# A fused linear-attention and mixture-of-experts kernel: unpermuted decay tiles, split copies and long probability rows in the first chunk

## The chip, the cores and the metric

The kernel runs on one core of one Trainium2 chip. The metric is device microseconds (us) of one execution; a profiled execution also has a span, about 1.7 us shorter, measured from the core's first instruction to its last. Engines: PE = TensorE (matmul), PEld = its weight load, DVE = VectorE, ACT = ScalarE, POOL = GpSimd, SP = SyncE, which here only issues DMA transfers. Runs over 1.5% above the fastest of the same kernel are called slow.

## The reference, cut to what matters

```python
f = 1 / (1 + exp(-f_logit))                       # q, k, v, f_logit: 4 x 8 x 768 x 48
for t in range(768):                               # per batch and head
    state = f[t][:, None] * state + outer(k[t], v[t])
    y[t] = q[t] @ state
x = y, heads side by side                          # 3072 x 384
p = domain_probs / (domain_probs.sum(-1) + 1e-9)   # 3072 x 4
out = sum_e p[:, e] * (relu(x @ w1[e]) @ w2[e])    # w1: 4 x 384 x 1024, w2: 4 x 1024 x 384
```

## The kernel before

The sequence is cut into six chunks of 128 positions; each chunk has 4 batches. Attention of a chunk feeds the expert matmuls of the same chunk. A list planner in Python orders all work by estimated costs and emits it; the chip then runs each engine's list in that order. The first expert matmul ("first MoE matmul" below) needs the transposed attention output of all four batches of chunk 0, and the first expert weight. The parts that matter here:

```python
# loads of chunk 0, one per tensor and batch, 192 KB each, all issued by SyncE, in this order
"f0 k0 q0 f1 k1 q1 f2 f3 k2 q2 v0 k3 q3 v1 v2 v3"
...
def load_w(i, e, which):                           # eight weight loads, issued by GpSimd
    ins["w", i] = nc.gpsimd.dma_start(out=w[:, e], in_=r[e])
    if i == 0:
        after(ins["w", 0], ins[0, "k", B - 1])     # released by the last key load
...
def load_p(c):                                     # six small loads, 16-byte pieces
    nc.sync.dma_start(out=p_dst[:, :, c], in_=p_src[:, :, c])
...
for o in done:                                     # fillers keep TensorE busy until the MoE starts
    for _ in range(o.pad):
        nc.tensor.matmul(out=spare[:, 0:256], lhsT=busy[:, 0:128], rhs=busy, start=True, stop=True)
    o.emit(o.engine)
```

## Time and profile before

| | before |
|---|---|
| median of the first 3 runs | 303.09 us (301.59 to 309.10) |
| profiled run, span | 302.06 us, 300.4 us |
| TensorE busy | 290.7 us (97%) |
| first weight lands | 23.05 us |
| first MoE matmul | 23.10 us |
| all timed runs of this kernel (g_before_again apart) | 56; 17 of them over 307 us |

The table reads as a start of 23.1 us, then an almost gapless run of TensorE.

### The profile page before, as it was taken

To read this page: it belongs to the slowest core of one execution; us is meant where nothing else is said; L and a number is where in the kernel's file an instruction comes from. 1 tells how busy PE (TensorE), PEld (TensorE's weight loads), DVE (VectorE), ACT (ScalarE), POOL (GpSimd) and SP (SyncE) were. 2 spreads that over 40 slices of the span, in tenths; PEclk is the share of its full clock that TensorE was granted. 3 is DMA by queue.
4 is the path that set the end of the run, shared out by engine and by line. 5 is a ranking of instruction groups with operands and counts; after the bars stand their busy time and mean duration, and the time that the engine had idled before them with its cause. 6 is when DMAs were issued, how large, how long until landed. Compare 5 with 4: busy or idle time off the path is not lost.

```text
span 300.4 us, 5514 instructions
## 1 busy us (share of the span) xinstructions
PE 290.7 (97%) x2111; PEld 168.1 (56%) x2141; DVE 135.8 (45%) x268; ACT 172.5 (57%) x300; POOL 95.7 (32%) x157
## 2 busy tenths in 40 slices
PE   7799999999999999999999999999999999999995
PEld 5564555567775565555555555555555555555553
DVE  6784013787852675516465325454415343201223
ACT  5766654858875455677355576445475444475440
POOL 4484400408756048423426243522432000000000
PEclk9999999999999999999999999999999999999999
DMA  7999999964994679969796978201322201200002
GB/s 155 210 180 206 207 207 200 220 103 71 224 208 103 119 142 180 196 136 156 152 177 116 241 147 153 49 21 34 94 58 52 48 13 41 75 4 2 0 0 105
DMA packets 137354, 36.08 MB, mean 120 GB/s; under 512 B 128496, under 2 KB 135792, under 8 KB 137328
## 3 DMA queue, kind: packets, MB, share of 16 engines
q1 hardware_dynamic: 131568, 29.45, 50.5%
q0 software_dynamic: 5760, 6.29, 12.6%
q8 instruction: 16, 0.26, 0.4%
q14 instruction: 10, 0.08, 0.1%
HBM read 31.51 MB, written 4.72 MB: 121 GB/s over the span
## 4 chain that ended last, share of the span: by engine, by line
PE 90%; DMA 4%; SPq 3%; DVE 1%; issue 1%
PE ps_m L356 42%; PE ps_m L344 41%; SPq L222 3%; DMA w_sb<-in_moe_w_dram 3%; PE ps_t L300 2%; DMA k<-in_k_dram 1%; PE ps_t L315 1%; PE ps_t L311 1%; PE ps_t L321 1%; PE ps_t L255 1%; PE ps_t L285 1%; DVE Sf L328 0%; DVE o L367 0%; DVE yb L218 0%; PE ps_t L340 0%
## 5 line engine op out<-in xcount | busy, mean ns | idle before, releaser
L356 PE MATMUL ps_m<-w_sb,h 128*128 128x384 bf16 x776 | 153.1, 324 | 0.2
L344 PE MATMUL ps_m<-xT,w_sb 128*128 128x512 bf16 (+1 forms) x594 | 150.8, 362 | 2.4 <-DMA w_sb<-in_moe_w_dram 0.5
L352 ACT ACTIVATE h<-ps_m 128x512 bf16<-128x512 f32 (+1 forms) x169 | 97.2, 577 | 96.5 <-PE ps_m L344 91.8
L356 PEld LDWEIGHTS <-h 128*128 128x128 bf16 x776 | 73.6, 98 | 58.7
L363 DVE SCALAR_TENSOR_TENSOR o<-ps_m,pn,o 128x384 f32<-128x384 f32 (+1 forms) x73 | 44.6, 611 | 107.3 <-PE ps_m L356 102.7
L344 PEld LDWEIGHTS <-w_sb 128*128 128x128 bf16 x624 | 59.5, 98 | 46.8 <-issue 0.8
L276 POOL TENSOR_TENSOR qk<-q,e 128x384 bf16<-128x384 f32 x19 | 22.8, 1202 | 67.3 <-ACT e L262 64.8
L335 POOL TENSOR_TENSOR Sf<-Sf,egs 48x192 f32<-48x192 f32 x40 | 20.1, 502 | 47.1 <-DVE Sf L328 45.1
L350 DVE TENSOR_SCALAR h<-ps_m 128x512 bf16<-128x512 f32 (+1 forms) x39 | 21.9, 578 | 27.6 <-PE ps_m L344 25.2
L304 DVE TENSOR_TENSOR AT<-ps_t,mask 128x512 bf16<-128x512 f32 x48 | 30.2, 682 | 6.8 <-PE ps_t L300 6.8
L276 POOL TENSOR_TENSOR qk<-k,e 128x384 bf16<-128x384 f32 x20 | 21.9, 1093 | 10.7 <-ACT egs L266 6.6
L262 ACT ACTIVATE e<-ps_t 128x384 f32<-128x384 f32 x24 | 20.8, 865 | 3.6 <-PE ps_t L255 2.5
L328 DVE TENSOR_TENSOR Sf<-Sf,ps_t 48x192 f32<-48x192 f32 x40 | 14.0, 350 | 8.3 <-PE ps_t L321 7.4
L336 POOL CAST sb<-Sf 48x192 bf16<-48x192 f32 x40 | 13.6, 339 | 2.6
L365 ACT ACTIVATE o<-ps_m,pn 128x384 f32<-128x384 f32 x20 | 11.6, 580 | 4.4 <-PE ps_m L356 3.2
L569 PE MATMUL ps_m<-busy 128*128 128x256 bf16 x69 | 12.1, 319 | 1.3 <-DVE busy L140 1.3
L264 ACT ACTIVATE e<-ps_t 128x384 f32<-128x384 f32 x24 | 13.0, 542 | 0.0
L247 ACT ACTIVATE ex<-f 128x768 f32<-128x768 f32 (+1 forms) x14 | 10.5, 750 | 4.4 <-DMA f<-in_f_logit_dram 4.4
L315 PE MATMUL ps_t<-vb,AT 128*128 128x48 bf16 x192 | 11.4, 184 | 1.0 <-DVE vb L218 1.0
L218 POOL CAST vb<-v 128x384 bf16<-128x384 f32 x18 | 9.4, 540 | 8.5 <-DMA v<-in_v_dram 7.3
L315 PEld LDWEIGHTS <-AT 128*128 128x128 bf16 x192 | 9.8, 97 | 3.1 <-issue 1.1
L251 ACT ACTIVATE gp<-ex 128x768 bf16<-128x768 f32 (+1 forms) x14 | 10.5, 752 | 0.4
(50 smaller groups left out, 134.5 us busy)
## 6 DMA issues: line engine op xcount, KB each, us to landing
w_sb<-in_moe_w_dram POOLq DMA_DIRECT2D x8, 768.0 KB, 18.9
out_dram<-o SPq DMA_DIRECT2D x23, 192.0 KB, 2.1
f<-in_f_logit_dram SPq DMA_DIRECT2D x10, 384.0 KB, 4.3
k<-in_k_dram SPq DMA_DIRECT2D x10, 384.0 KB, 5.5
q<-in_q_dram SPq DMA_DIRECT2D x10, 384.0 KB, 5.4
v<-in_v_dram SPq DMA_DIRECT2D x10, 384.0 KB, 5.1
f<-in_f_logit_dram SPq DMA_DIRECT2D x4, 192.0 KB, 4.0
k<-in_k_dram SPq DMA_DIRECT2D x4, 192.0 KB, 4.1
```

Of the source, the lines that this page charges most:

```text
L262: nc.scalar.activation(out=e[:, 0].rearrange("t (d h) -> t h d", d=D), in_=cs[:, 0:HD].rearrange("t (i r d) -> t r i d", r=2, d=D), func=A ...
L276: engines[eng].tensor_tensor(out=tl("qk", c, b)[:, j, :, 0:D].rearrange("t (i r) d -> t i r d", r=2), in0=tl("qk"[j], c, b // 2)[:, hh(b), ...
L304: nc.vector.tensor_tensor(out=tl("AT", c, b)[:, r].rearrange("s i t -> s (i t)"), in0=tl("A", c, b, r).rearrange("s i t -> s (i t)"), in1= ...
L315: nc.tensor.matmul(out=y[:, h * D:(h + 1) * D], lhsT=AT[:, r, i, :], rhs=vb[:, h, :], start=(c == 0), stop=True, skip_group_check=True)
L328: nc.vector.tensor_tensor(out=Sf[rows, b], in0=Sf[rows, b], in1=KV[rows, :, r, :], op=ALU.add)
L335: nc.gpsimd.tensor_tensor(out=Sf[rows, b], in0=Sf[rows, b], in1=eg, op=ALU.mult)
L336: nc.gpsimd.tensor_copy(out=nb[rows, b, :, r * D:(r + 1) * D], in_=Sf[rows, b])
L344: nc.tensor.matmul(out=tl("hp", c, e, fc, n0)[:, n0:n1], lhsT=w1_sb[:, e, kk, fc * 128:(fc + 1) * 128], rhs=tl("xT", c)[:, kk, n0:n1], sta ...
L350: nc.vector.tensor_relu(out=dst, in_=src)
L352: nc.scalar.activation(out=dst, in_=src, func=AF.Relu)
L356: nc.tensor.matmul(out=tl("op", c, e, nt, part)[:, cols], lhsT=tl("h", c, e)[:, fc, nt * T:(nt + 1) * T], rhs=w2_sb[:, e, fc, cols], start ...
L363: nc.vector.scalar_tensor_tensor(out=o, in0=op, scalar=pe, in1=o, op0=ALU.mult, op1=ALU.add)
```

## The change

Its intent is to shorten the attention of chunk 0 and to replace the six small probability loads. The release of the weights by the last key load stays as it was.

```diff
-    nc.sync.dma_start(out=p_dst[:, :, c], in_=p_src[:, :, c])          # six times
+    nc.scalar.dma_start(out=praw, in_=moe_domain_probs.rearrange("(r p) e -> r p e", p=T))   # once, at the start
+    nc.tensor.transpose(out=tl("pp")[:, e], in_=praw[:, :, e], identity=ident32)             # x4, fp32
...
-    nc.scalar.activation(out=e[:, 0].rearrange("t (d h) -> t h d", d=D), in_=cs..., func=AF.Exp, scale=-1.0)
+    if c == 0:
+        nc.scalar.activation(out=e[:, 0], in_=cs[:, 0:HD], func=AF.Exp, scale=-1.0)
+    else: ...                                                            # as before
...
-            pe = {"DVE": 0.6, "POOL": 1.0} if c < 2 else {"POOL": 1.0}
+            pe = {"DVE": 0.55} if c == 0 and b == B - 1 else {"DVE": 0.55, "POOL": 1.36} if c == 0 else ...
...   (the last batch's copies of QK, y and xT in two parts, ScalarE and VectorE)
+            parts = [slice(0, KD)] if c or b < B - 1 else [slice(0, 2), slice(2, KD)]
...
-                    add_load(c + 2, nm, 2 * half, 2, u0 + 30 + 4 * half + j)
+                    add_load(c + 2, nm, 2 * half, 2, u0 + 30 + 4 * half + j, deps=[wd[5]])
```

More of the change, by code (lines that the diff above doesn't have):

```diff
@@ L167 @@
         Sb.append(t)
-    pt = const.tile([128, B * C, E], FP32)
-    pn = const.tile([128, B * C, E], FP32)
-    psm = const.tile([128, B * C, 1], FP32)
+    NR = B * C
+    praw = const.tile([NR, T, E], FP32)
+    ident32 = const.tile([NR, NR], FP32)
+    nc.vector.tensor_copy(out=ident32, in_=ident[0:NR, 0:NR])
+    pn = const.tile([T, E, NR], FP32)
+    psm = const.tile([T, NR], FP32)
     w1_sb = wpool.tile([128, E, KD, F], BF16)
@@ L186 @@
         "cs": ([T, 512], FP32), "tp": ([128, 2, NP, T], BF16), "A": ([T, NP, T], FP32), "y": ([T, 512], FP32),
-        "KV": ([T, 512], FP32), "xp": ([T, KD, T], BF16), "hp": ([128, NT], FP32), "op": ([128, 512], FP32),
+        "KV": ([T, 512], FP32), "xp": ([T, KD, T], BF16), "hp": ([128, NT], FP32), "op": ([128, 512], FP32), "pp": ([T, E, NR], FP32),
     }
@@ L192, in tl @@
         if (kind, key) not in tiles:
-            room = kind if kind in rooms else "ps_m" if kind in ("hp", "op") else "ps_t"
+            room = kind if kind in rooms else "ps_m" if kind in ("hp", "op", "pp") else "ps_t"
             slot = P.slot[(room, kind) + key if room.startswith("ps_") else (room,) + key]
@@ L231, in load_w, with load_p, pe_pp, probs @@
             after(ins["w", 0], ins[0, "k", B - 1])
-    p_src = moe_domain_probs.rearrange("(b c p) e -> p b c e", p=128, c=C)
-    p_dst = pt.rearrange("p (b c) e -> p b c e", c=C)
-    def load_p(c):
-        nc.sync.dma_start(out=p_dst[:, :, c], in_=p_src[:, :, c])
-    def probs(c):
-        t, s, n = (x.rearrange("p (b c) e -> p b c e", c=C)[:, :, c] for x in (pt, psm, pn))
-        nc.vector.tensor_reduce(out=s, in_=t, axis=mybir.AxisListType.X, op=ALU.add)
-        nc.vector.tensor_single_scalar(out=s, in_=s, scalar=1e-9, op=ALU.add)
-        nc.vector.reciprocal(out=s, in_=s)
-        nc.vector.tensor_tensor(out=n, in0=t, in1=s.broadcast_to([128, B, E]), op=ALU.mult)
+    def load_p():
+        nc.scalar.dma_start(out=praw, in_=moe_domain_probs.rearrange("(r p) e -> r p e", p=T))
+    def pe_pp():
+        for e in range(E):
+            nc.tensor.transpose(out=tl("pp")[:, e], in_=praw[:, :, e], identity=ident32)
+    def probs():
+        nc.vector.tensor_reduce(out=psm, in_=tl("pp").rearrange("p e r -> p r e"), axis=mybir.AxisListType.X, op=ALU.add)
+        nc.vector.tensor_single_scalar(out=psm, in_=psm, scalar=1e-9, op=ALU.add)
+        nc.vector.reciprocal(out=psm, in_=psm)
+        nc.vector.tensor_tensor(out=pn, in0=tl("pp"), in1=psm.unsqueeze(1).broadcast_to([T, E, NR]), op=ALU.mult)
     def gate1(c, b, n):
@@ L261, in exps @@
         cs, e = tl("cs", c, b), tl("e", c, b)
-        nc.scalar.activation(out=e[:, 0].rearrange("t (d h) -> t h d", d=D), in_=cs[:, 0:HD].rearrange("t (i r d) -> t r i d", r=2, d=D),
-                             func=AF.Exp, scale=-1.0)
+        if c == 0:
+            nc.scalar.activation(out=e[:, 0], in_=cs[:, 0:HD], func=AF.Exp, scale=-1.0)
+        else:
+            nc.scalar.activation(out=e[:, 0].rearrange("t (d h) -> t h d", d=D),
+                                 in_=cs[:, 0:HD].rearrange("t (i r d) -> t r i d", r=2, d=D), func=AF.Exp, scale=-1.0)
         nc.scalar.activation(out=e[:, 1], in_=cs[:, 0:HD], func=AF.Exp)
@@ L274, in product @@
         e = tl("e", c, b)[:, j]
-        e = e.rearrange("t (d r i) -> t i r d", d=D, r=2) if j == 0 else e.rearrange("t (i r d) -> t i r d", d=D, r=2)
+        e = e.rearrange("t (d r i) -> t i r d", d=D, r=2) if j == 0 and c > 0 else e.rearrange("t (i r d) -> t i r d", d=D, r=2)
         engines[eng].tensor_tensor(out=tl("qk", c, b)[:, j, :, 0:D].rearrange("t (i r) d -> t i r d", r=2),
@@ L336, in state, with pe_xt @@
             nc.gpsimd.tensor_copy(out=nb[rows, b, :, r * D:(r + 1) * D], in_=Sf[rows, b])
-    def pe_xt(c, b):
-        for kk in range(KD):
-            nc.tensor.transpose(out=tl("xp", c, b)[:, kk, :], in_=tl("yb", c, b)[:, kk * 128:(kk + 1) * 128], identity=ident)
+    def pe_xt(c, b, ks):
+        for kk in range(ks.start, ks.stop):
+            nc.tensor.transpose(out=tl("xp", c, b, ks.start)[:, kk, :], in_=tl("yb", c, b)[:, kk * 128:(kk + 1) * 128], identity=ident)
     def mm_h(c, e, fc, n0, n1):
@@ L360, in ev_o @@
         op, o = tl("op", c, e, nt, part)[:, cols], tl("o", c, nt)[:, cols]
-        pe = pn[:, nt * C + c, e:e + 1]
+        pe = pn[:, e, nt * C + c:nt * C + c + 1]
         if e > 0:
@@ L416, in attention @@
                        deps=[G[b]], takes=[pt_("cs")], lag=0.2, frees=[("gp", c, half)])
-            ex = P.add(f"exps {c}.{b}", {"ACT": 0.98 if c else 1.1}, on(exps), s(0) + 0.1, deps=[cs],
+            ex = P.add(f"exps {c}.{b}", {"ACT": 0.98 if c else 1.0}, on(exps), s(0) + 0.1, deps=[cs],
                        takes=[("e", c, b)] + ([("egs", c, b)] if c == 0 else []), frees=[pt_("cs")])
@@ L420, in attention @@
                             frees=[("e", c, b)], lag=2.0) if c and more else None)
-            pe = {"DVE": 0.6, "POOL": 1.0} if c < 2 else {"POOL": 1.0}
+            pe = {"DVE": 0.55} if c == 0 and b == B - 1 else {"DVE": 0.55, "POOL": 1.36} if c == 0 else {"DVE": 0.6, "POOL": 1.0} if c == 1 else {"POOL": 1.0}
             qm = P.add(f"q {c}.{b}", pe, one(product, 0), s(4) - 0.2,
@@ L425, in attention @@
                        deps=[ex, ld[c, "k", b]], takes=[("qk", c, b)], frees=[("k", c, half), ("e", c, b)])
-            vb = P.add(f"v {c}.{b}", {"ACT": 0.52, "DVE": 0.36} if c == 0 else {"POOL": 0.5, "ACT": 0.52} if c == 1 else {"POOL": 0.5}, one(cast_v), s(4),
+            vb = P.add(f"v {c}.{b}", {"ACT": 0.52} if c + b == 0 else {"ACT": 0.52, "DVE": 0.36} if c == 0 else {"POOL": 0.5, "ACT": 0.52} if c == 1 else {"POOL": 0.5}, one(cast_v), s(4),
                        deps=[ld[c, "v", b]], takes=[("vb", c, b)], frees=[("v", c, half)])
@@ L432, in attention @@
                            takes=[pt_("tp")], frees=[("qk", c, b)], lag=0.2)
-                et = P.add(f"ev_tp {c}.{b}", {"DVE": 0.69, "ACT": 1.05}, lambda e, b=b: copy(e, tl("QK", c, b)[0:MP], tl("tp", c, b)[0:MP]), s(4) + 0.1,
-                           deps=[tq, tk], takes=[("QK", c, b)], frees=[pt_("tp")])
-            else:
-                et = P.add(f"tp {c}.{b}", {"DMA": 1.8}, on(dma_tp), s(4), deps=[qm, km], takes=[("QK", c, b)],
-                           frees=[("qk", c, b)], lag=2.2)
+                parts = [(slice(0, 2), [tq, tk])] if c or b < B - 1 else [(slice(j, j + 1), [tj]) for j, tj in enumerate((tq, tk))]
+                et = [P.add(f"ev_tp {c}.{b}", {"DVE": 0.69, "ACT": 1.05} if len(parts) == 1 else {"DVE": 0.37, "ACT": 0.55},
+                            lambda e, b=b, js=js: copy(e, tl("QK", c, b)[0:MP, js], tl("tp", c, b)[0:MP, js]), s(4) + 0.1,
+                            deps=ds, takes=[("QK", c, b)], frees=[pt_("tp")]) for js, ds in parts]
+            else:
+                et = [P.add(f"tp {c}.{b}", {"DMA": 1.8}, on(dma_tp), s(4), deps=[qm, km], takes=[("QK", c, b)],
+                            frees=[("qk", c, b)], lag=2.2)]
             ET[b], VB[b] = et, vb
@@ L443, in attention @@
             at = P.add(f"at {c}.{bs[-1]}", {"PE": 0.43 if len(bs) == 1 else 0.66}, lambda e, bs=bs: [pe_at(c, b) for b in bs], slot(bs[-1], 7),
-                       deps=[ET[b] for b in bs], takes=[("ps_t", "A", c, b, r) for b in bs for r in range(2)], lag=0.2,
+                       deps=[t for b in bs for t in ET[b]], takes=[("ps_t", "A", c, b, r) for b in bs for r in range(2)], lag=0.2,
                        frees=[("QK", c, b) for b in bs])
@@ L457, in attention @@
             Y.append(y)
-            ey = P.add(f"ev_y {c}.{b}", {"ACT": 0.48, "DVE": 0.56},
-                       lambda e, b=b: copy(e, tl("yb", c, b), tl("y", c, b)[:, 0:HD]), s(11) + 0.1,
-                       deps=[y], takes=[("yb", c, b)], frees=[pt_("y")])
-            if c < 2:
-                xt = P.add(f"xt {c}.{b}", {"PE": 0.17}, on(pe_xt), s(13), deps=[ey],
-                           takes=[pt_("xp")], frees=[("yb", c, b)], lag=0.2)
-                xdone[c, b] = P.add(f"ev_xt {c}.{b}", {"ACT": 0.48, "DVE": 0.4},
-                                    lambda e, b=b: copy(e, tl("xT", c)[:, :, b * T:(b + 1) * T], tl("xp", c, b)),
-                                    s(13) + 0.1, deps=[xt], takes=[("xT", c)], frees=[pt_("xp")])
-            else:
-                xdone[c, b] = P.add(f"xt {c}.{b}", {"DMA": 0.9}, on(dma_xt), s(13), deps=[ey], takes=[("xT", c)],
-                                    frees=[("yb", c, b)], lag=2.2)
+            parts = [slice(0, KD)] if c or b < B - 1 else [slice(0, 2), slice(2, KD)]
+            cs_ = lambda ks: slice(ks.start * 128, ks.stop * 128)
+            ey = [P.add(f"ev_y {c}.{b}", {"ACT": 0.48, "DVE": 0.56} if len(parts) == 1 else {"ACT": 0.4, "DVE": 0.4},
+                        lambda e, b=b, ks=ks: copy(e, tl("yb", c, b)[:, cs_(ks)], tl("y", c, b)[:, cs_(ks)]), s(11) + 0.1,
+                        deps=[y], takes=[("yb", c, b)], frees=[pt_("y")]) for ks in parts]
+            if c < 2:
+                xdone[c, b] = []
+                for ks, eyk in zip(parts, ey):
+                    xt = P.add(f"xt {c}.{b}", {"PE": 0.17}, on(pe_xt, ks), s(13), deps=[eyk],
+                               takes=[pt_("xp", ks.start)], frees=[("yb", c, b)], lag=0.2)
+                    xdone[c, b].append(
+                        P.add(f"ev_xt {c}.{b}", {"ACT": 0.48, "DVE": 0.4} if len(parts) == 1 else {"ACT": 0.36, "DVE": 0.3},
+                              lambda e, b=b, ks=ks: copy(e, tl("xT", c)[:, ks, b * T:(b + 1) * T], tl("xp", c, b, ks.start)[:, ks]),
+                              s(13) + 0.1, deps=[xt], takes=[("xT", c)], frees=[pt_("xp", ks.start)]))
+            else:
+                xdone[c, b] = [P.add(f"xt {c}.{b}", {"DMA": 0.9}, on(dma_xt), s(13), deps=ey, takes=[("xT", c)],
+                                     frees=[("yb", c, b)], lag=2.2)]
             X.append(xdone[c, b])
@@ L474, in attention @@
             s15 = slot(b, 15) if c else 2 + 2 * b
-            kv = P.add(f"kv {c}.{b}", {"PE": 0.22}, on(pe_kv), s15, deps=[Y[b], X[B - 1] if c == 0 else None],
+            kv = P.add(f"kv {c}.{b}", {"PE": 0.22}, on(pe_kv), s15, deps=[Y[b]] + (X[B - 1] if c == 0 else []),
                        takes=[pt_("KV")], frees=[("vb", c, b), ("qk", c, b)], lag=0.2)
@@ L489, in add_h @@
         m = P.add(f"h {c}.{e}.{fc}.{n0}", {"PE": 0.645 * n / NT}, lambda _: mm_h(c, e, fc, n0, n1), p,
-                  deps=[wd[e, 1]] + [xdone[c, b] for b in xs], takes=[key], lag=0.2, frees=[("xT", c)])
+                  deps=[wd[e, 1]] + [t for b in xs for t in xdone[c, b]], takes=[key], lag=0.2, frees=[("xT", c)])
         hdone[c, e, fc, n0] = P.add(f"relu {c}.{e}.{fc}.{n0}",
@@ L509, in add_o @@
                                        lambda g: ev_o(c, e, nt, part, cols, g), p - 1,
-                                       deps=[m, oev.get((c, e - 1, nt)), pdone[c]], takes=[("o", c, nt)], frees=[key])
+                                       deps=[m, oev.get((c, e - 1, nt)), pdone], takes=[("o", c, nt)], frees=[key])
             if e == E - 1:
@@ L514 @@
     attention(0, lambda b, s: -200 + 3.6 * b + s * 0.8, 1)
+    pl = P.add("ld p", {"ACT": 0.1}, lambda e: load_p(), -1100, lag=3.0)
+    pp = P.add("pp", {"PE": 0.6}, lambda e: pe_pp(), -1, deps=[pl], takes=[("ps_m", "pp")], lag=0.2)
+    pdone = P.add("probs", {"DVE": 0.9}, lambda e: probs(), 4, deps=[pp] + xdone[0, B - 1], frees=[("ps_m", "pp")])
     ALL, LO, HI = list(range(B)), [0, 1], [2, 3]
@@ L530, in ol @@
         return [(c, e, nt, half) for nt in nts for half in range(2)]
-    pdone = []
     for c in range(C):
         u0 = unit[0]
-        pl = P.add(f"ld p{c}", {"DMA": 0.5}, lambda e, c=c: load_p(c), -900 if c == 0 else u0 - 6, lag=2.0)
-        pdone.append(P.add(f"probs {c}", {"DVE": 0.8}, lambda e, c=c: probs(c), u0 + 4, deps=[pl, xdone[c, B - 1]]))
         if c == 0:
```

## The prediction

> **What bounds the kernel now.** I first read the page's busy shares and the chain that ended last, because they say which engine sets the end.
>
> ```profile
> span 300.4 us, 5514 instructions
> PE 290.7 (97%) x2111; PEld 168.1 (56%) x2141; DVE 135.8 (45%) x268; ACT 172.5 (57%) x300; POOL 95.7 (32%) x157
> PE 90%; DMA 4%; SPq 3%; DVE 1%; issue 1%
> ```
>
> TensorE (PE) is busy 97% of the span and is 90% of the chain; the two MoE matmul lines alone (L356 41.8%, L344 40.5%) carry over four fifths. Nothing in the diff removes an MoE matmul, so the question is the part of the chain that is not TensorE: 4% DMA and 3% issue of loads. The chain in order of time shows that they all lie before the first MoE matmul:
>
> ```profile
> 9.16 0.82 SPq L222
> 10.03 4.38 DMA k<-in_k_dram
> 14.72 8.33 DMA w_sb<-in_moe_w_dram
> 23.54 1.03 PE ps_m L344 x4
> ```
>
> Columns: start, duration, what. The last key load lands at 10.03 + 4.38 = 14.41 us; that releases the first expert-weight load, issued at 14.72 and landing 8.33 us later, at 23.05; TensorE starts the MoE at 23.10. Then I read the timeline around that start, to see how much later the weights are than the attention that feeds the same matmul:
>
> ```profile
> 21.06 0.56 DVE L218 CAST yb<-ps_t 128x384 bf16<-128x384 f32 x1 [0.44 <-PE ps_t L315]
> 21.85 0.71 PE L569 MATMUL ps_m<-busy 128*128 128x256 bf16 x5
> 22.05 0.48 ACT L216 COPY xT<-ps_t 128x384 bf16<-128x384 bf16 x1 [0.74 <-PE ps_t L340]
> 23.09 0.98 PEld L344 LDWEIGHTS <-w_sb 128*128 128x128 bf16 x6 [0.81 <-DMA w_sb<-in_moe_w_dram]
> 23.10 1.47 PE L344 MATMUL ps_m<-xT,w_sb 128*128 128x512 bf16 x5 [0.54 <-DMA w_sb<-in_moe_w_dram]
> ```
>
> The last transposed attention block is copied out at 22.05 + 0.48 = 22.53. So the two inputs of the first MoE matmul are ready at 22.53 (attention) and 23.05 (weights): the weights end the wait, by 0.52 us. Whatever shortens the attention of the first chunk alone is worth nothing.
>
> After 23.10 the profile leaves almost no idle TensorE time: in windows from 25 to 250 us its idle time adds to 1.8 us (0.58 of it between 60 and 100 us), and after its last matmul at about 297.2 us only the last scale-and-add and stores remain. The span is therefore about 23.1 of start, 274.1 of matmul, 3.2 of tail.
>
> **What the Trainium skill says.** "DMA: Bandwidth & Descriptors", section "Issuing engines are not separate DMA queues": loads started by different engines run on the same 16 DMA engines and interleave; another issuing engine saves only sequencer time. This trace agrees: with loads issued by SyncE alone, and later with GpSimd's weights alone, the windows show the same 205 to 210 GB/s written (the weights are read as fp32 and written as bf16). Moving the probabilities to ScalarE's queue thus moves the bytes and does not hide them. The same page, section "Queues, rings and completion order", says that each DMA engine takes turns between its queues packet by packet. The trace fits: the small probability load of 8 KB, issued at 14.82 behind the last values, took 10.5 us to land, while the weights were moving. "SBUF — State Buffer", section "SBUF: two separate sides", says that VectorE and GpSimd lock a shared port for the whole instruction. The trace agrees: the VectorE cast of v at 13.42, 0.34 us when undisturbed, took 1.07 us, beside a GpSimd product running from 12.79 to 14.27; and weight issues by GpSimd run beside a VectorE that never idles.
>
> **The change, part by part.**
>
> 1. Unpermuted decay tiles in chunk 0. In the groups of the first 23 us the permuted ScalarE exponential has 862 ns, the plain one 536 ns: 4 x 0.326 = 1.3 us off ScalarE. The VectorE q product that reads the permuted tile has 854 ns, the k product that reads a plain one 540 ns: 4 x 0.314 = 1.26 us off VectorE.
>
> 2. Last batch split. The v cast of batch 0 goes to ScalarE alone (0.34 off VectorE). From the last mask multiply, ending at 18.75 + 1.87 = 20.62, to 22.53, the tail is 1.91 us. With halves at the sizes that the diff's own planner gives (0.40, 0.36), the three links shrink from 0.56, 0.34, 0.48 to about 0.40, 0.22, 0.36: 0.40 us. VectorE had no gap from 14.4 to 20.62, so its savings after the last key load count on this path: q product of batch 3 (0.31) and about one cast (0.34). Sum 1.05: attention ready at about 22.53 - 1.05 = 21.5. It had 0.52 us of slack already; it gets 1.0 more and none of it reaches TensorE directly.
>
> 3. Probabilities as 24 rows of 2 KB, once, at the start, instead of six loads of 512 pieces of 16 bytes. Cost: 49 KB in the first loads; at 207 GB/s that is 0.24 us, which could push the last key load from 14.41 to at most 14.65. Gain: no 512 small packets beside the first weights. From the loads, 1024 pieces of 192 bytes per 0.95 us, a piece costs an engine about 15 ns, so 32 pieces per engine are at most 0.48 us; they were served until 25.3, so perhaps half to all of them fell before 23.05. The 18 to 22 us window moved 191 GB/s against 206 afterwards: had the same 764 KB gone at 206, they would take 3.71 instead of 4.0 us, 0.29 us. Four fp32 transposes of 24 rows are added on TensorE; like the other small ones (about 0.2 us each with pipelining) they fit its filler time at about 6 us. The six chains of four small VectorE operations (about 0.7 us each) become one; VectorE is at 45% and they were not waited for, except 0.5 us once by ScalarE.
>
> 4. Release of the weights. In both versions the weights wait for the last key load; the diff changes no line of that. The new dependency of later loads on the sixth weight load orders the planner only: the third chunk's first load was issued at 71.42 anyway, long after that weight had landed (42.29).
>
> Sum on the path: +0.1 to +0.24 (key load later) - 0.3 (cleaner first weights) gives about 0 to -0.3 us; I take -0.25, first MoE matmul near 22.85. The rest of TensorE's 274 us stays, give or take 0.3 from the changed order.
>
> **The rivals.** First, the weights could land earlier by about 1 us, because the release or the descriptor writing on GpSimd speeds up with a less crowded VectorE (the 16.8 to 18.0 us window moves only 83 GB/s, a real dip between loads and weights worth 0.7 us). Then attention at 21.5 bounds: gain up to 1.2 to 1.5 us, 301.0. For it: the dip; against: nothing in the diff aims at it and VectorE stays nearly full there. Second, the extra early load and the in-order wait of TensorE on the probability transposes could delay chunk 0: if those rows land after about 7.2 us, the first q transposes wait. ScalarE can issue only after its table load at 2.08, other loads take 4.1 us to landing, so 6.2 to 6.7 is likely; a slip of 0.5 us would be absorbed by the attention's slack, and only a late key load costs, up to 0.3 us: 302.5. Third, the list planner re-orders everything after any cost changes, and a PSUM room for MoE is held by the transposed probabilities until attention ends; an unlucky order could open 1 to 2 us of TensorE gaps: 303.5. Against it, matmul time is long and VectorE is idle from 21.6 on, so the room comes back before it is needed.
>
> **Range and chances.** The three runs before are 301.59, 303.09 and 309.10 and the profiled one 302.06; the 309.10 is an outlier, and the fast level is about 302.3 (mean of the other three). Less 0.25: 302.05, called 302.1. The spread of runs, about 0.8 to each side, and the rivals give 300.7 to 304.0. Two per cent is 6 us; no term comes near it, and only a disturbed median would: faster 0.02, same 0.96, slower 0.02.
>
> **What would show it right or wrong.** Right: the chain again runs through key load and first weight load; the weight's landing is at 22.6 to 23.1 and the first MoE matmul right behind it; the last copy of the transposed block ends at 21.2 to 21.9; the plain exponentials and q products of chunk 0 are near 0.54 us; TensorE busy near 290. Wrong: a first MoE matmul before 22.3 (first rival) or after 23.4 (second), the chain going through attention instead of weights, or TensorE idle over 3 us between 25 and 297 us (third).

## The result, and the profile after

The changed kernel took 313.41 us (313.11 to 314.05, 6 runs); the kernel before in the same rounds 302.5 us median (301.59 to 312.73, 6 runs). The ratio is 1.0379, interval 1.0353 to 1.0404. (A ratio here is the mean time of one kernel's fast runs over that of the other's of the same rounds, so not quite the ratio of the medians.) It is slower by 3.8%, and by nearly the amount by which the slow runs of before are slow.

The page of the changed kernel, busy shares and chain:

```profile
span 311.7 us, 5491 instructions
PE 291.9 (94%) x2107; PEld 169.4 (54%) x2137; DVE 131.2 (42%) x250; ACT 170.2 (55%) x302; POOL 94.9 (30%) x157
PE 86%; DMA 5%; SPq 4%; DVE 2%; issue 1%; ACT 0%; DVEq 0%
```

TensorE is as busy as before (291.9 against 290.7 us); the span grew around it. The chain in order of time (start, duration, what; pieces between left out) shows where:

```profile
13.51 0.90 SPq L225
14.45 15.01 DMA v<-in_v_dram
29.49 0.03 ACT vb L219
29.91 0.47 ACT xT L219
31.31 0.32 PE ps_t L322 x8
34.38 2.32 PE ps_m L351 x10
```

The chain no longer goes through the key load and the first weight. It goes through the last v load (v3, the sixteenth): issued at 14.45, it lands 15.01 us later, at 29.46. In the kernel before, ScalarE began its cast of the last v at 18.80. The timeline of the changed kernel shows what waits for it, and the weights' issue:

```profile
14.45 2.03 SPq L225 DMA_DIRECT2D v<-in_v_dram  x1
15.15 6.77 POOL L232 DMA_DIRECT2D w_sb<-in_moe_w_dram  x8 [1.23 <-DMA k<-in_k_dram]
29.49 0.51 ACT L219 CAST vb<-v 128x384 bf16<-128x384 f32 x1 [10.22 <-DMA v<-in_v_dram]
30.81 0.50 PE L347 MATMUL ps_t<-ident,yb 128*128 128x128 bf16 x3 [10.27 <-ACT yb L219]
33.78 2.92 PE L351 MATMUL ps_m<-xT,w_sb 128*128 128x512 bf16 x11
```

ScalarE stands idle 10.22 us until v lands, TensorE behind it 10.27 us, and the first MoE matmul starts at 33.78 instead of 23.10: 10.7 of the 11.3 us by which the span grew. The first weight had landed long before: its load took 7.4 us from its issue at 15.15, so 22.55. Note also the issue of the last v: 2.03 us, where the kernel before has the first of these lines (the second is its cast of the last v):

```profile
13.87 0.90 SPq L222 DMA_DIRECT2D v<-in_v_dram  x1
18.80 0.51 ACT L216 CAST vb<-v 128x384 bf16<-128x384 f32 x1 [0.38 <-DMA v<-in_v_dram]
```

The windows of one microsecond of the changed kernel (stretch, its length, busy time and count of PE, PEld, DVE, ACT, POOL, then the granted clock, DMA share, GB/s) show the stretch in which nothing runs but DMA:

```profile
22.00:23.00 1.00, 0.00 (x0) 0.00 (x0) 0.00 (x0) 0.00 (x0) 0.00 (x0) 1.00 1.18 211
24.00:25.00 1.00, 0.00 (x0) 0.00 (x0) 0.00 (x0) 0.00 (x0) 0.00 (x0) 0.50 1.13 203
33.00:34.00 1.00, 1.00 (x9) 0.77 (x7) 0.90 (x5) 0.11 (x1) 0.00 (x0) 0.50 1.16 219
```

The DMA engines move about 200 GB/s all the while: they carry weights. The granted clock falls to half some 3.3 us after TensorE went idle (20.55) and is back at about 34, which makes the tail of attention slower too (three transposes at 30.81 took 0.50 us, those of the last batch before, at 21.68, 0.34). The Trainium skill, "TensorE: Matmul & The Clock Gate", section "Part 1: The HAM clock gate (the "warmup" mystery)", gives about 3.4 us of idleness for that fall; this trace agrees. It also explains why this kernel's runs have a lower mean clock (0.981 to 0.983): TensorE was idle 3.3 us before the clock fell, so the low clock is a consequence of the gap, not its cause. The listed slow runs of the kernel before have 0.978 to 0.989, which fits the same reading but was not seen in a profile.

**Packets.** The trace holds every DMA packet with its start, size and queue. I counted them per microsecond: "v" are the 192-byte pieces of SyncE's loads (chunk 0 has 16 x 1024), "w" the pieces of the weights.

```
 us      before: v sent, of 16384 | w sent      changed: v sent, of 16384 | w sent
 15-16        1103   (15382)          0                975   (14455)          0
 16-17         905   (16287)          8                830   (15285)          8
 17-18          70   (16357)         28                 75   (15360)         24
 18-19          27   (16384)         81                  0   (15360)         86
 19-20           -                   90                  0   (15360)        100
 21-22           -                  113                 95   (15493)         97
 23-24           -                  103                 92   (15682)         86
 25-26           -                  162                 94   (15862)         93
 27-28           -                  254                191   (16239)        192
```

Before, the first weight piece went at 16.62, and at 17 us only 97 v pieces were left. In the changed kernel, at 18 us exactly one load, 1024 pieces, had not begun. From 20 us on it goes piece for piece with the weights, 95 against 97, and a weight piece has 2048 bytes (768 later) where a v piece has 192. At that rate 1024 pieces need about 10 us. The starts of single pieces show the same: from 21 to 24.5 us, 300 of 311 weight pieces and 306 of 324 v pieces are followed by a piece of their own kind 178 ns later (within 2.5 ns; at other distances it is typically a third), so an engine serves one of each in about 0.18 us, and 16 engines make some 90 of each per us. The load is not slow, it is served one small piece for each large one.

### The profile page after: what moved, and what is told of

It reads as the page before. It is cut to its first block, busy times and chain, and to the rows that moved or that the text cites. A ratio compares the mean times of both kernels' runs of the same rounds, so it can differ in the third digit from the quotient of the medians.

```text
span 311.7 us, 5491 instructions
## 1 busy us (share of the span) xinstructions
PE 291.9 (94%) x2107; PEld 169.4 (54%) x2137; DVE 131.2 (42%) x250; ACT 170.2 (55%) x302; POOL 94.9 (30%) x157
## 4 chain that ended last, share of the span: by engine, by line
PE 86%; DMA 5%; SPq 4%; DVE 2%; issue 1%; ACT 0%; DVEq 0%
PE ps_m L363 40%; PE ps_m L351 39%; DMA v<-in_v_dram 5%; SPq L225 4%; PE ps_t L307 2%; PE ps_t L322 1%; DVE qk L283 1%; PE ps_t L318 1%; PE ps_t L328 1%; PE ps_t L259 1%; PE ps_t L292 1%; PE ps_t L347 0%; PE ps_m L583 0%; ACT xT L219 0%; DVE o L370 0%
## 5 line engine op out<-in xcount | busy, mean ns | idle before, releaser
L359 ACT ACTIVATE h<-ps_m 128x512 bf16<-128x512 f32 (+1 forms) x171 | 98.7, 580 | 101.3 <-PE ps_m L351 92.8
L283 POOL TENSOR_TENSOR qk<-q,e 128x384 bf16<-128x384 f32 x18 | 21.3, 1185 | 63.9 <-ACT e L269 58.8
L357 DVE TENSOR_SCALAR h<-ps_m 128x512 bf16<-128x512 f32 (+1 forms) x37 | 20.2, 559 | 25.8 <-PE ps_m L351 17.9
L269 ACT ACTIVATE e<-ps_t 128x384 f32<-128x384 f32 x20 | 17.3, 865 | 3.3 <-PE ps_t L259 2.7
L583 PE MATMUL ps_m<-busy 128*128 128x256 bf16 x61 | 13.4, 357 | 1.3 <-DVE busy L140 1.3
L271 ACT ACTIVATE e<-ps_t 128x384 f32<-128x384 f32 x24 | 12.8, 533 | 0.0
L347 PE MATMUL ps_t<-ident,yb 128*128 128x128 bf16 x24 | 3.0, 240 | 10.3 <-ACT yb L219 10.3
L251 ACT ACTIVATE ex<-f 128x768 f32<-128x768 f32 (+1 forms) x14 | 10.5, 747 | 3.3 <-DMA f<-in_f_logit_dram 3.3
L221 DVE CAST yb<-ps_t 128x384 bf16<-128x384 f32 (+1 forms) x9 | 4.9, 542 | 14.0 <-PE ps_t L322 13.9
```

The source lines that it names most:

```text
L269: nc.scalar.activation(out=e[:, 0].rearrange("t (d h) -> t h d", d=D), in_=cs[:, 0:HD].rearrange("t (i r d) -> t r i d", r=2, d=D), func=A ...
L283: engines[eng].tensor_tensor(out=tl("qk", c, b)[:, j, :, 0:D].rearrange("t (i r) d -> t i r d", r=2), in0=tl("qk"[j], c, b // 2)[:, hh(b), ...
L357: nc.vector.tensor_relu(out=dst, in_=src)
L359: nc.scalar.activation(out=dst, in_=src, func=AF.Relu)
```

## The experiments

Theory A: the last v load is starved by the weights because the weights arrive in the DMA rings before it is through. Theory E, formed after the first four runs: what makes it late is TensorE's instruction fetch. In the trace a queue of kind "instruction" moves 16 pieces of 16 KB; the Trainium skill, "Runtime: NRT & Kernel Launch", section "Instruction fetch mechanics", says that an engine's instructions are refilled in blocks of 16 KiB, 256 instructions, by a DMA queue of its own. 16 or 17 blocks fit TensorE's instructions (4266 in the trace before, 4259 in that of the changed kernel) and no other engine's (384 at most), so I take it as TensorE's; the trace does not name it. Counting bears this out: from one fetch to the next TensorE starts 252 instructions on average in both traces, near the 256 of a block, and no other engine more than 23 on average. The first of these fetches begins at 16.13 us before and at 14.62 us in the changed kernel.

All results, fast and slow runs listed together; "last v" is the last load of v, and its first and last piece are those of the last 1024 in order of time:

| run | fetch begins | last v: issue us | its first piece | first weight piece | its last piece | times, us |
|---|---|---|---|---|---|---|
| before | 16.13 | 0.90 | 15.98 | 16.62 | 18.38 | 39 of 56 at 301.4 to 305.1, 17 at 308.0 to 313.8 |
| g_before_again | 16.20 | 0.93 | 16.12 | 16.97 | 19.36 | 303.76 |
| changed | 14.62 | 2.03 | 20.24 | 16.80 | 29.03 | 313.1 to 314.1 |
| p12_noprobs | 14.45 | 2.30 | 20.13 | 16.31 | 28.95 | 314.7 to 315.6 |
| p3_probs (slow run) | 15.01 | 2.38 | 20.46 | 16.86 | 29.16 | 303.3, 303.4, 314.4, 315.2 |
| d_rel_q | 14.83 | 2.26 | 17.54 | 18.16 | 18.99 | 303.6 to 304.9 |
| c_rel_v | 14.94 | 2.08 | 17.55 | 21.37 | 18.94 | 306.1 to 307.4 |
| e_wide_fill | 16.87 | 0.92 | 16.93 | 17.80 | 19.35 | 303.0 to 304.2 |
| p12_wide | 16.82 | 1.10 | 16.63 | 17.16 | 20.34 | 304.1, 304.2, 306.7, 306.9 |
| f_before_more_fill | 12.79 | 0.63 | 17.35 | 17.98 | 18.57 | 303.2 to 304.9 |
| j_few_more | 17.32 | 1.02 | 16.96 | 17.50 | 23.93 | 306.8, 308.9, 313.4, 315.6 |
| h_late_p | 16.97 | 0.93 | 16.88 | 17.69 | 19.30 | 303.1 to 305.1 (4), 309.1, 310.6 |
| k_late_p_rel_q | 17.02 | 1.09 | 16.88 | 17.95 | 19.42 | 303.6 to 304.4 (6) |
| n_fp32_fill | 16.74 | 1.02 | 16.88 | 17.67 | 19.19 | 303.2 to 303.6 (6) |
| o_fp32_rel_q | 17.00 | 0.99 | 16.85 | 17.95 | 19.47 | 303.7 to 304.8 (6) |
| r_before_rel_q | 16.00 | 0.88 | 16.03 | 17.13 | 18.32 | 302.6 to 303.8 (6) |
| s_rel_q_split | 15.92 | 0.74 | 16.02 | 17.10 | 18.10 | 302.1 to 303.8 (6) |
| t_rel_k_split | 15.77 | 0.89 | 15.93 | 16.56 | 18.13 | 301.9 to 302.5 (4), 304.1, 306.8 |

All sixteen experiments gave correct results. The table's middle columns are of the one profiled run of each.

### First round: release and parts

**d_rel_q**, the changed kernel with one wait altered; the order on every engine is the same:

```diff
-            after(ins["w", 0], ins[0, "k", B - 1])
+            after(ins["w", 0], ins[0, "q", B - 1])
```

> The changed kernel with one wait altered: the weights wait for the last q load instead of the last key load; every engine's order is the same. Theory A (the weights are released while SyncE is still issuing the last v load, and what is left of that load is then served behind the weights): the release comes about 1 us later, the last v issue is over by then, the last v lands in under 6 us instead of 15.0, the first weight lands near 23.4, the span is near 301.5 and the time near 303. Rival B (the last v load is starved because weights and values share the DMA engines at all, however they are ordered): it still takes 12 us or more and the time stays at 311 to 314.

Measured: 304.34 us median, none slow; ratio to before 1.0059 (1.002 to 1.0098). The last v's last piece went at 18.99 instead of 29.03. That one wait, about 1 us later, removed nearly all of the loss. Theory A held and rival B fell; the time came out 1.3 us above the figure I had given. The first MoE matmul is back at 23.49, and it waits for the first weight:

```profile
19.60 0.51 ACT L219 CAST vb<-v 128x384 bf16<-128x384 f32 x1
23.49 1.68 PE L351 MATMUL ps_m<-xT,w_sb 128*128 128x512 bf16 x6 [0.23 <-DMA w_sb<-in_moe_w_dram]
```

**c_rel_v**, the same with "v" (and the planner told so).

> The changed kernel with the weights released by the last v load, so that no weight packet is in flight with the first chunk's loads. Theory A and rival B both expect the last v to land in 4 to 5 us at about 18.8, the first weight then some 7.4 to 8.3 us after its issue, at 26.5 to 27.3, and a time of 305.5 to 307: better than the 313.4 of the change, worse than before. Rival C (the loss is not the starved v load but the changed order of the attention work): stays above 311.

Measured: 306.59 us. The chain is the expected one, with the first weight as the bound:

```profile
14.61 4.82 DMA v<-in_v_dram
19.73 7.13 DMA w_sb<-in_moe_w_dram
27.15 1.06 PE ps_m L351 x2
```

The last v lands in 4.82 us, yet its issue took 2.08 us with no weight in flight: so the long issue is not made by the weights. Rival C fell.

**p3_probs**, the kernel before with the probabilities' part alone, and **p12_noprobs**, the changed kernel with the probabilities as before (decay tiles and split copies alone). The edits are those of the diff above, one part each.

> The kernel before with only the probabilities changed (long rows, loaded at the start by ScalarE's queue, transposed on TensorE). Theory A: this early load alone pushes SyncE's later issues by about 0.5 us and starves the last v load: 311 to 314, last v in flight about 15 us. Rival D (the trigger is the attention part: faster ScalarE and VectorE work and another split over GpSimd): about 302, last v in flight 5 us.

> The changed kernel with the probabilities as before (six small loads, none early), so only the decay tiles and the split of the last batch are new. Theory A: last v lands as before (about 5 us in flight), weights land at 23.05 as before and bound the start, attention is ready at 21.3 to 21.9: time 301.5 to 302.5, no different from before. Rival D: 311 to 314 with the last v starved.

Measured: p3_probs 303.3, 303.4, 314.4 and 315.2 us; p12_noprobs 314.91 us, all four at 314.7 to 315.6, ratio 1.0414 (1.0385 to 1.0443). I had the parts the wrong way round. The attention part alone does it in all four runs (which of its edits was not tried); the early load alone does it in half the runs, hardly another share than the kernel before (5 of 9 in that round). So the mechanism of theory A stood, but not its trigger.

### Second round: what makes the last v late

In the five kernels of this table with a long last v issue (2.03 to 2.38 us), the instruction fetch begins at 14.45 to 15.01, within that issue each time; where it begins at 15.77 or later the issue takes 0.74 to 1.10. My guess was that the faster attention brings TensorE to the fetch point earlier. The traces speak against it: by 14.62 us TensorE had started 196 instructions in the kernel before and 196 in the changed one, so why the fetch comes 1.5 us earlier stays open. The traces of all eighteen profiles also give the order that separates the full starvation from the rest: in its three cases (changed, p12_noprobs, p3_probs) SyncE ended the issue of the last v 0.41 to 0.86 us after GpSimd had ended that of the first weight, in the other fifteen 0.45 us or more before. To test the link with the fetch I moved the fetch without touching the attention.

**e_wide_fill**, the changed kernel; **p12_wide**, the same edit on p12_noprobs:

```diff
-    busy = wk.tile([128, 256], BF16, name="busy")
+    busy = wk.tile([128, 512], BF16, name="busy")
-        for _ in range(o.pad):
-            nc.tensor.matmul(out=spare[:, 0:256], lhsT=busy[:, 0:128], rhs=busy, start=True, stop=True)
+        for w in [512] * (o.pad // 2) + [256] * (o.pad % 2):
+            nc.tensor.matmul(out=spare[:, 0:w], lhsT=busy[:, 0:128], rhs=busy[:, 0:w], start=True, stop=True)
```

> The changed kernel with one thing altered: two filler matmuls of 256 columns become one of 512, so TensorE is kept as busy with some 36 fewer instruction rows before 14.6 us. Theory E: TensorE's first fetch of a 16 KB block of instructions (at 14.62 us in the changed kernel, 16.13 in the one before) occupies a DMA engine for 1.4 us, holds SyncE in the issue of the last v load (2.03 us instead of 0.90), and so lets the weights get ahead of it. With fewer rows the fetch moves to 16 us or later, the last v issue takes 0.8 to 1.1 us, the last v lands in 4 to 6 us, the first MoE matmul is at 22.5 to 23.2, the time 301 to 303. Rival F (the starving depends on the attention order or on GpSimd's earlier release, not on the fetch): the last v stays 15 us in flight and the time at 313 to 315.

> The attention part of the change without its probabilities (314.9 us), with the fillers made half as many and twice as wide. Theory E: fetch after 16 us, last v issue about 0.9 us, time 301 to 303; if the weights also have the small probability load beside them, the first weight lands some 0.2 to 0.5 us later than in the wide-filler run of the whole change. Rival F: 314 to 315.

Measured: e_wide_fill 303.27 us (302.99 to 304.17), ratio to before 1.0015 (0.9964 to 1.0067), none slow; fetch at 16.87, last v issue 0.92. Fillers of another shape, with no part of the change undone, took 10 us off the changed kernel. The release was not later: the first weight was issued at 15.13 against 15.15. (Its first piece still went 1.0 us later, for a reason that no run shows; so the fillers moved more than the fetch.) p12_wide came to 304.1 to 306.9: the issue was normal (1.10), but the last piece of v went at 20.34, so it was still partly in the alternation. The starvation was cut, not always gone; the expected 301 to 303 was too good.

**f_before_more_fill** goes the other way on the kernel before: the first 20 fillers are each split into two of half the width.

```diff
+            split = 2 if fills < 20 else 1
+            fills += 1
+            for _ in range(split):
+                nc.tensor.matmul(out=spare[:, 0:256 // split], lhsT=busy[:, 0:128], rhs=busy[:, 0:256 // split], ...)
```

> The kernel before with its first 20 filler matmuls each split into two of half the width: 40 more instruction rows early, the same TensorE time. Theory E: the first instruction fetch moves from 16.13 to about 14.5 us, into the issue of the last v load, which becomes 2.0 to 2.4 us long and is starved: all runs near 309 to 314 (before has some of each). Rival F: the mix of fast and slow runs stays that of before (about half at 302 to 305).

Measured: 303.7 us, all four fast. The expectation missed, because the fetch went to 12.79, not 14.5. There it fell into an earlier issue (that of v1, 1.90 us from 12.37), and the last key load, already under way, landed at 15.39 instead of 14.41, so the weights were issued later too (15.70) and the order was kept. In this run the fetch did no harm, because the release was late as well.

**g_before_again**, the kernel before, unaltered.

> The kernel before, unaltered, to see a profile of its other state if it comes up. Theory E: if the run is near 302, the instruction fetch begins after 15.7 us and the last v is in flight under 6 us; if it is at 308 to 313, the fetch falls into the issue of the last v load or the weights come before it, and the last v is in flight 9 us or more.

It ran at 303.76, so the other state was not caught. It shows a mild case: the last piece of v at 19.36, a microsecond later than in the first profile, and 1.7 us more time.

### Third round: timing of the fetch, and a later probability load

**j_few_more** is f_before_more_fill with 10 splits instead of 20.

> The kernel before with its first 10 filler matmuls split in two (20 more rows; the run with 40 more moved the fetch to 12.79 us, ahead of the last loads). Theory E: the fetch now begins between 13.5 and 15 us, inside or just ahead of the last v issue; that issue takes 1.8 to 2.4 us, the last v is 9 us or more in flight, and all or nearly all runs are at 308 to 314. If the fetch falls at 13 us or earlier, or at 15.5 us or later, the last v lands in under 7 us and the runs are at 302 to 305. Rival F: a mix as in before wherever the fetch falls.

Measured: 306.8, 308.9, 313.4 and 315.6 us. The fetch came at 17.32, which I had not foreseen: the number of instructions alone does not give its time. The last v issue was normal, and yet the load was late, as the chain of waits of the 308.9 us run shows:

```profile
13.98 0.70 SPq L222
14.73 9.71 DMA v<-in_v_dram
24.46 0.03 ACT vb L216
```

So theory E in its first form, "the fetch lengthens the issue", is too narrow. Here the fetch began 0.36 us after the first piece of the last v, and took 0.93 us, and the weights began at 17.50. A fetch piece that held the DMA engine it lies on would leave that engine's share of v behind, to be served at one piece per weight piece: at 95 pieces per us over 16 engines, about 6 per us and engine, the 64 pieces of one engine would need up to 10 us. That is an estimate from the counts above. It fits 23.93. The counts of this run go some way: 53 pieces of v were left at 20 us and went at 18, 18, 11 and 6 per us, by that estimate the rates of three engines down to one, where the changed kernel had 95. So here a few engines were behind, not all. The trace does not say on which engine a packet ran, so that the fetch put them there is not shown.

**h_late_p** is e_wide_fill with the probabilities loaded by SyncE behind the last v and transposed during the first MoE matmuls; **k_late_p_rel_q** is h_late_p with the weights released by the last q load.

```diff
-        nc.scalar.dma_start(out=praw, ...)
+        nc.sync.dma_start(out=praw, ...)
-    pl = P.add("ld p", {"ACT": 0.1}, lambda e: load_p(), -1100, lag=3.0)
+    pl = P.add("ld p", {"DMA": 0.3}, lambda e: load_p(), -900, lag=9.0)
```

> The wide-filler version of the change with the long-row probabilities loaded by SyncE behind the last v load, and transposed on TensorE during the first MoE matmuls. The early load had put the last key load at 14.8 to 14.9 us instead of 14.4 to 14.5. Expected: last key load and weight release 0.4 us earlier, fetch at 16 us or later, last v issue about 0.9 us, last v 4 to 6 us in flight, first MoE matmul 22.5 to 23.0, time 301.5 to 302.5, no slow run. If the last v issue is again held by the fetch: 309 or more in some or all runs.

> The same with the weights released by the last q load instead of the last key load, so that nearly all of the last v load is through before the first weight packet. Expected: release 0.9 to 1.0 us later, at 15.4 to 15.6; last v in flight under 5 us whatever the fetch does; attention ready at 21.3 to 22.0, first weight at 22.8 to 23.3 and the bound; time 301.8 to 302.8 with no run over 304. Rival: no gain over the run without this wait, or 0.5 us worse, if the last v was not in the way there.

Measured: h_late_p 303.1 to 305.1 in four runs, 309.1 and 310.6 in two; k_late_p_rel_q 303.57 to 304.42 in all six. The late probability load gave nothing I could see, and the slow runs are back where the release is the key load's. With the q load's release they are gone, and the first weight is the bound, as the chain of k_late_p_rel_q has it:

```profile
11.81 4.08 DMA q<-in_q_dram
16.20 7.73 DMA w_sb<-in_moe_w_dram
23.98 0.61 PE ps_m L351 x2
```

### Fourth round: with or without the fetch; the release on the kernel before

**n_fp32_fill**: h_late_p with four fillers replaced by one fp32 filler; **o_fp32_rel_q**: the same with the q load's release; **r_before_rel_q**: the kernel before with only that release.

```diff
+        for w in [256] * (o.pad // 4):
+            nc.tensor.matmul(out=spare[:, 0:w], lhsT=busy32[:, 0:128], rhs=busy32[:, 0:w], start=True, stop=True)
```

> The late-probabilities version with four fillers of 256 columns replaced by one fp32 filler (one instruction row instead of eight): some 20 to 50 fewer rows early than in any run so far, so that TensorE's first instruction fetch should begin at 18 us or later, behind all of the first chunk's loads. Theory E: with no fetch between 12 and 18 us no engine falls behind, the last v's last packet is at 18.0 or earlier (19.30 in the same version with the fetch at 16.97), attention is ready at 21.8 to 22.6, the first weight is the bound at 22.5 to 23.0, all runs at 301.5 to 302.8 and none over 304 (the same version with the fetch at 16.97 had 2 of 6 above 309). Rival G (the closeness of the weight release to the last v is enough, without the fetch): 1 to 3 of 6 runs at 308 or more again.

> The same with the weights released by the last q load. Both theories: no slow run, first weight 0.8 to 1.1 us later than without, at 23.3 to 23.9, time 302.5 to 304; a control for what safety by a later release costs.

> The kernel before with only the release altered to the last q load. If the slow runs of the kernel before (308 to 313, some third of all) are the same starved load: none of the runs is over 304.5, and all lie at 302.8 to 304 because the first weight comes about 1 us later than 23.05. If the slow runs have another cause: 1 to 3 of 6 at 308 or more, as before.

Measured: n_fp32_fill 303.42 us, six fast runs, but the fetch stayed at 16.74, so the run did not test what it was made for: whether the fetch is needed stays open. The trace shows why: each fp32 filler stands in it as two matmuls and two weight loads, so TensorE has 4238 instructions, as many as in h_late_p. o_fp32_rel_q took 303.94 us, so the later release cost 0.5 us, less than the 0.8 to 1.1 expected. r_before_rel_q took 303.16 us with all six runs between 302.64 and 303.81, while the kernel before in the same round had 2 of 12 at 312. Against the fast runs of before it is 1.0024 (1.0003 to 1.0045); over all runs its mean is 303.25 against 304.17. Its TensorE waited for the first weight:

```profile
PE ps_m L344 <- DMA w_sb<-in_moe_w_dram: 1.4, 1, 1.4
```

### Fifth round: a smaller first weight

**s_rel_q_split** and **t_rel_k_split**: the kernel before, with the first weight as two loads of 512 columns, released by the last q load and by the last key load.

```diff
-        ins["w", i] = nc.gpsimd.dma_start(out=w[:, e], in_=r[e])
+        parts = 2 if i == 0 else 1
+        n = w.shape[3] // parts
+        for p in range(parts):
+            one = nc.gpsimd.dma_start(out=w[:, e, :, p * n:(p + 1) * n], in_=r[e][:, :, p * n:(p + 1) * n])
+            if p == 0:
+                ins["w", i] = one
```

> The kernel before with the weights released by the last q load and the first expert's first weight loaded as two halves of 512 columns (1 KB packets). If the account is right, the later release removes the starving (no run over 304.5), and the first half lands some 1.5 to 2 us before the whole did (23.53 in the version without halves, where attention was ready at 22.15): first MoE matmul at 22.1 to 22.6 instead of 23.58, time 301.5 to 302.5. Rival: the halves share the engines with the next weights, the first half gains under 0.5 us, time 302.8 to 303.8.

> The kernel before with only the halves, released by the last key load as before. Packets of half the size halve the price of each place in the alternation, so a starved last v load would cost half as much: first weight at about 21.5, so that the last v (18.4 to 20 us) and the attention bound the start at 22.3 to 23, time 301.5 to 302.5 in most runs; slow runs, if any, at 305 to 308 instead of 308 to 314. If the release by the key load is what makes slow runs possible, 1 to 3 of 6 are slow here, none with the release by the q load.

Measured: s 302.73 us (302.11 to 303.83), t 302.27 us (301.93 to 306.75); before in the same round 302.05 us, with 3 of 11 at 312.4 to 312.8. The first MoE matmul of s started at 22.11 against 23.58 in r_before_rel_q, as expected. But the span is 301.1, not the 299.4 that a start 1 us earlier than in the kernel before would give. The chain of s shows where the gain went:

```profile
20.66 21.62 DMA w_sb<-in_moe_w_dram
42.30 11.02 DMA f<-in_f_logit_dram
53.35 0.85 ACT ex L252
54.22 0.85 ACT gp L256
```

TensorE waited 1.7 us for chunk 1's first gate at about 55 us. The loads of chunk 1 are issued when the sixth weight has landed, at 42.3, and its first f load lands only at 53.3. An earlier start just meets this wait. In t the outlying runs are 304.14 and 306.75: up to 4.5 us above its median, where slow runs of before lay 10.4 us or more above theirs. That fits a price per place halved with the piece, but two runs are few, and in another round a slow run of before lay only 5.1 us above the median.

## Why the prediction was wrong

**What held.** "The weight's landing is at 22.6 to 23.1" was 22.55, just below, and partly by luck: the weight was issued 0.43 us later and took 7.4 us instead of 8.33, each more than foreseen, and the two misses cancel in part. The plain exponentials were 0.49 us and the q products 0.54 to 0.56 in undisturbed cases. TensorE's busy time was 291.9. The later issue (15.15 against 14.72) is nearly twice the 0.24 I had allowed for the early load; with the probabilities of before (p12_noprobs) it was 14.67. Two slips changed nothing: +0.1 to +0.24 less 0.3 is -0.06 to -0.2, not -0.25, and ScalarE issued the probability load at 0.83, not after its table load at 2.08.

**The step that failed** is the second rival's last sentence: "a slip of 0.5 us would be absorbed by the attention's slack, and only a late key load costs". I took a late load as costing what it is late. The last v load costs something else: little while nearly all of it is through before the weights begin, and some 10 us once it is behind. So the bound that I had, the first weight with 0.5 us of slack for the attention, was the wrong one: the first MoE matmul waited for attention and started at 33.78, not near 22.85. I had the evidence: I quoted that a probability load of 8 KB behind the last v took 10.5 us to land, and read it as a fact about probabilities. It lay one place behind v in the same queue. The packet count shows how close the kernel before was: when its first weight piece went (16.62), 369 of 16384 pieces of v were left. Releasing the weights 1 us later (d_rel_q) brought 304.3 us, and that is the test of this step.

**A second step failed** more quietly: "attention ready at about 22.53 - 1.05 = 21.5". Without any starving (d_rel_q) the last copy ended at 22.93, and in e_wide_fill at 23.19. The values set it: in d_rel_q the cast of v2 began at 18.98, after VectorE had waited 1.09 us for its load, and that of v3 at 19.60. In e_wide_fill the last v, 5.45 us in flight, is on the chain itself. Saving VectorE and ScalarE time ahead of a load that lands then is worth nothing. The split copies gave little too: from the end of the last mask multiply to the last copy d_rel_q took 1.79 us against 1.91, where 0.40 less was expected. This is part of why even without the accident the change is at 303.3 us and not ahead of before: the first MoE matmul of e_wide_fill starts at 23.47, 0.4 of the 0.8 us by which its span is longer.

**The third thing** I passed over was in the given times: 309.10 among three runs was called "an outlier". In the runs of this study 17 of 56 of that kernel are slow. Of the runs whose weights were released by the last q or v load none was slow: 32 of 32, twelve of them of the kernel before with that release. I take the slow runs of before as the same accident, because that release removes them (with 5 of 23 slow in the same rounds, twelve fast ones in a row would come by chance about once in twenty); no slow run of the unaltered kernel before was profiled.

**What is settled and what not.** Shown: the loss is the starved last v load; the release decides it. Shown for the changed kernel: fewer and wider fillers move the instruction fetch and end it, in four runs of four (with the same fillers h_late_p was slow in two of six). That the fetch is the link between the two is inferred from its time in the eighteen profiles. It is not a rule: of the SyncE issues after 40 us in all eighteen, 46 of the 92 in which a fetch begins take over 1.85 us (as all six such in the first chunk's loads do), against 170 of the 1699 without one, and a long issue is also more likely to contain a fetch. Not settled: whether the fetch is needed in every case (j_few_more was starved with a normal issue, n_fp32_fill did not move it); why it comes earlier in the changed kernel; and why the starved load stood still for about 2 us (17.98 to 20.24) before its first piece, while in d_rel_q it began at once.

**No version beat both kernels** clearly. The fast runs of before remain the fastest by 0.2 to 0.3%. For steadiness, r_before_rel_q and s_rel_q_split trade that for having no slow runs (means over all runs 303.25 against 304.17, and 302.87 against 304.83).

## What to carry to other kernels

When a bulk transfer is released by a load that is not the last of its group, look at what is still in flight then: a load of small pieces is cheap while alone and may be served one small piece per large one afterwards, so its cost is a step, not a slope. A run that is an "outlier" by 2 to 4% with a lower clock can be such a step that the kernel sometimes falls over; profile it before changing anything near it. And a saving ahead of the bound should be followed to the next wait: here a start 1 us earlier met chunk 1's loads at 55 us.

## What the Trainium skill lacked or had wrong

- "DMA: Bandwidth & Descriptors", section "Queues, rings and completion order", says that an engine drains a whole packet of about 9 to 17 descriptors from one ring before it switches. Here the alternation was piece for piece, one of each per engine in about 0.18 us: 94 pieces of 192 bytes beside 93 of 2048 bytes in one microsecond, and 191 beside 192 when the weight pieces had 768 bytes. That a load of small pieces is therefore starved (15.0 us for 192 KB that took 4.82 in c_rel_v, with no weight in flight) is not on the page.
- "Runtime: NRT & Kernel Launch", section "Instruction fetch mechanics", calls the crossing of a 16 KiB boundary mostly hidden. The fetch pieces took 0.9 to 1.8 us each, and where one began at 14.45 to 15.01 us, in the first chunk's loads, SyncE's issue of the last v took 2.0 to 2.4 us instead of 0.6 to 1.1, in five kernels of five. That the fetch is the cause is inferred.
- No page that I found says that the filler matmuls move such a fetch in time, and that their shape can decide a race between loads: the fetch began at 14.62 us and the time was 313.4 us with fillers of 256 columns, 16.87 and 303.3 with 512. Their number alone does not give its time (on the kernel before, 16.13; with 10 fillers split in two 17.32, with 20 split 12.79).
